# Loading all token tiles at once, normalising them in place on ScalarE, and passing keys, queries, maxima and heads through DRAM in few DMAs

## The chip, the cores and the metric

The kernel runs on one core of a Trainium2 chip. The metric is the device time of one execution in microseconds, as a median of several runs. TensorE is called PE here, VectorE DVE, ScalarE ACT, GpSimd POOL and SyncE SP, as in the profile.

## What is computed

A layer norm, then attention with 32 heads of 16 columns, gated by a bilinear feed-forward layer, all in float32 on 2048 tokens of 512 columns:

```python
xn = _layernorm(x, axis=-1)
# attention: H = 32, Dh = 16
qkv = (xn @ wqkv).reshape(B, S, 3, H, Dh)      # then q, k, v by head
p = softmax(einsum("bhqd,bhkd->bhqk", q, k) * Dh ** -0.5)
s = einsum("bhqk,bhkd->bhqd", p, v) @ wo
# gate: F = 1792
h = (xn @ w_gate) * (xn @ w_up)
g = silu(h @ w_down)
return x + s * g
```

## The kernel before

Most products are made from float32 values split in a high part (rounded) and a low part (the remainder); a product is then three matmuls: high by high, high by low, low by high. Tokens stand in 16 tiles of 128 (`tt`), four to a chunk of 512 (`c`). Heads go in 8 groups of four (`g`); two groups come out of one projection of 128 columns (`m`). One unit of attention `i` is a group of heads with a chunk of queries, 32 units; each has 16 rounds, one for each tile of keys, so there are 512 rounds.

The main loop runs over the rounds. In each, `expo` makes four transposed score tiles (one for each head) and their exponentials on ACT, `score` makes four score tiles of a later unit for their maxima (`LEAD`, 21 rounds ahead), `pv` multiplies the exponentials with the values, and a `Filler` runs a share of the remaining projections, the feed-forward layer and the ending. A score contracts over 48 rows: for each head the keys are (high, low, high) of 16 rows each and the queries (high, high, low). Two rows more carry the negative maxima (high and low) on the queries' side against ones on the keys' side. Heads j = 0, 2 stand at partitions 0 to 49 and j = 1, 3 at 64 to 113 of the tiles `ks` and `QS`.

`qk_proj` and `proj_pair` make keys and queries; `qk_high` (L243) rounds the result on ACT, `qk_out` (L248) makes the low part on DVE and stores both: for each of the three groups of rows (`r`) one DMA to `KD` or `QD` in DRAM, laid out by head and row. `load_q` (L465) and `load_k` (L474) load them for a unit or a group, one DMA for each head. For the first heads (m = 0; all keys, and the first queries) `qk_out` writes directly from SBUF to `ks` and `QS`, in 12 DMAs of 16 rows. `maxima` (L494) sends the maxima through DRAM in 4 stores and 4 loads; `finish` (L531) stores the normalised heads in 4 DMAs.

Ahead of the main loop stands `early` (L561). It loads the token tiles into `raw_x` (8 places, whose tile later becomes the second keys' tile `ks1`), with the other eight loaded once a place is free; `ln_stats`, `ln_root`, `ln_scale` and `ln_apply` normalise (chunk 0 on DVE, the others on POOL, into tiles `xt`), `ln_turn` transposes on PE and splits into `xh` (ACT) and `xl` (DVE). Then a stream of 264 pieces, one 128-row matmul of 512 columns each, runs with an order written out by hand: keys, queries and values of the first heads, with the norm's steps of later chunks at given places (`at`), and at the places of `EARLY` a group of four scores (84 in all). The PSUM tags there are `s` (4 banks, scores), `x` (2, transposes) and `f` (2, projections).

The order of the instructions on PE, ACT and DVE is that of the program (`manual_schedule`); on SP and POOL a scheduler chooses it. SP issues all DMAs, in its order: one that waits holds those behind it.

Of the kernel before, what the change touches and what calls it, by code (L numbers as in the profile page):

```python
# [36 lines left out]
XBUFS = 7  # L37
EARLY = [44 + 16 * n for n in range(7)] + [156 + 8 * n for n in range(14)]
# [7 lines left out]
def body(ctx, tc, x, wqkv, wo, wg, wu, wd, out):  # L46
# [13 lines left out]
    KD = [dram.tile([8, KB, S], F32R, name=f"KD{m}") for m in range(NG // 2)]  # L60
    QD = [[dram.tile([8, KB, 512], F32R, name=f"QD{m}_{c}") for c in range(NC)] for m in range(NG // 2)]
    XD = [dram.tile([2, P, ND, 512], F32R, name=f"XD{c}") for c in range(NC)]
    MD = [dram.tile([32, P], F32, name=f"MD{i}") for i in range(NG * NC)]
    OD = [dram.tile([D, 512], F32, name=f"OD{c}") for c in range(NC)]
# [10 lines left out]
    nc.gpsimd.memset(V[:, :, DH:H * VW:VW], 1.0)  # L75
    nc.gpsimd.memset(V[:, :, H * VW:], 1.0)
# [65 lines left out]

    def load_x(tt):
        dma(raw_x[:, tt % 8], x[tt * P:(tt + 1) * P])

    def ln_stats(tt):
        c, t = divmod(tt, 4)
        if t == 0:
            norm[c] = [qp.tile([P, 4, 2], F32, name="mv", bufs=2)] + [qp.tile([P, 4], F32, name=n, bufs=2)
                                                                        for n in ("ve", "r0", "e1")]  # L150
        st = qp.tile([P, 6], F32, name="st", bufs=2)
        nc.vector.bn_stats(st, raw_x[:, tt % 8])
        nc.vector.bn_aggr(norm[c][0][:, t], st)

    def ln_root(c):
        mv, ve, r0, e = norm[c]
# [3 lines left out]
    def ln_scale(c):  # L160
        mv, ve, r0, e = norm[c]
# [4 lines left out]
        nc.vector.tensor_tensor(e, r0, e, op=OP.mult)  # L166

    def ln_apply(tt):
        c, t = divmod(tt, 4)
        mv, ve, r0, e = norm[c]  # L170
# [3 lines left out]
        norm[c, t] = xt  # L174

    def ln_turn(tt):
        c, t = divmod(tt, 4)
        xt = norm[c, t]
# [55 lines left out]
    def proj_pair(m, which):  # L234
# [6 lines left out]
        soon(1, lambda: [qk_out(o, hi, m, w, c) for o, hi, (_, w, c) in zip(outs, his, which)])  # L241

    def qk_high(o):  # L243
        hi = qp.tile([P, D], F32, name="xt", bufs=XBUFS).bitcast(F32R)
        fst["high"] = nc.scalar.activation(hi, o, AF.Copy)
        return hi

    def qk_out(o, hi, m, which, c):  # L248
        lo = qp.tile([P, D], F32, name="xt", bufs=XBUFS).bitcast(F32R)
        nc.vector.tensor_tensor(lo, o, hi, op=OP.subtract)  # L250
        sl = slice(c * 512, (c + 1) * 512)
        heads = slice(0, P)
        three = (hi, hi, lo) if which == 0 else (hi, lo, hi)
        if m == 0 and (which == 1 or c == 0):
            heads = slice(64, P)
            for j in range(4):
                for r, src in enumerate(three):
                    at = slice(64 * (j % 2) + r * DH, 64 * (j % 2) + (r + 1) * DH)
                    dmar(QS[0][at, j // 2] if which == 0 else ks[0][at, j // 2, sl], src[j * DH:(j + 1) * DH])
        dst = QD[m][c] if which == 0 else KD[m][:, :, sl]  # L260
        for r, src in enumerate(three):
            dmar(dst[heads.start // DH:, r * DH:(r + 1) * DH], src[heads])
# [87 lines left out]
    def o_split(c, tiles):  # L350

        for d, (oh, ol) in enumerate(tiles):
            n = P if c < NC - 1 or d < ND - 1 else 64
            raw = wtile(("w1r", "w0r")[d % 2]).rearrange("p d q -> p (d q)")
            dma(raw[:n], OD[c][d * P:d * P + n])
# [105 lines left out]

    def load_q(i):
# [3 lines left out]
        if i:  # L466
# [4 lines left out]
    def load_k(g):  # L471
        for j in range(4):
            b = 64 * (j % 2)
# [275 lines left out]
```

## Time and profile before

| | us |
|---|---|
| median of 3 runs (lowest, highest) | 1872.29 (1871.79, 1874.9) |
| profiled execution | 1870.86 |
| its span, first to last instruction | 1869.1 |
| PE busy | 1811.5 |
| DVE busy | 1489.6 |
| ACT busy | 1244.3 |
| POOL busy | 528.7 |

A profile has one execution's instructions with their times. PE is its matmuls, PEld its weight loads, which overlap with them. "Idle before" is an engine's idle time ahead of an instruction, with what ended it. PEclk is the share of the full TensorE clock that was granted. SPq means SP issuing DMAs.

### The profile page before, as it was taken

To read this page: it belongs to the slowest core of one execution; us is meant where nothing else is said; L and a number is where in the kernel's file an instruction comes from. 1 tells how busy PE (TensorE), PEld (TensorE's weight loads), DVE (VectorE), ACT (ScalarE), POOL (GpSimd) and SP (SyncE) were. 2 spreads that over 40 slices of the span, in tenths; PEclk is the share of its full clock that TensorE was granted. 3 is DMA by queue.
4 is the path that set the end of the run, shared out by engine and by line. 5 is a ranking of instruction groups with operands and counts; after the bars stand their busy time and mean duration, and the time that the engine had idled before them with its cause. 6 is when DMAs were issued, how large, how long until landed. Compare 5 with 4: busy or idle time off the path is not lost.

```text
span 1869.1 us, 34764 instructions
## 1 busy us (share of the span) xinstructions
PE 1811.5 (97%) x13560; PEld 1000.1 (54%) x13560; DVE 1489.6 (80%) x2461; ACT 1244.3 (67%) x2401; POOL 528.7 (28%) x549
## 2 busy tenths in 40 slices
PE   4799999999999999999999999999999999999998
PEld 3465555555555555555555555555555555555555
DVE  5478888888888888888888888888888888888822
ACT  1116777777777777777767677776777777767664
POOL 4120000042331324313322342331325314223451
PEclk8799999999999999999999999999999999999999
DMA  4231554441113122312113221130124111111232
GB/s 152 65 81 61 193 167 124 113 115 45 52 36 69 50 85 64 80 28 64 46 41 75 100 64 36 53 72 24 58 81 111 41 36 46 45 47 41 100 130 100
DMA packets 122504, 139.77 MB, mean 75 GB/s; under 512 B 18084, under 2 KB 79524, under 8 KB 119460
## 3 DMA queue, kind: packets, MB, share of 16 engines
q1 hardware_dynamic: 122340, 137.55, 25.5%
q8 instruction: 107, 1.75, 0.4%
q14 instruction: 57, 0.47, 0.1%
HBM read 93.98 MB, written 41.42 MB: 72 GB/s over the span
## 4 chain that ended last, share of the span: by engine, by line
PE 92%; ACT 2%; DVE 2%; SPq 1%; DMA 1%; issue 1%; POOL 0%; DVEq 0%; POOLq 0%; ACTq 0%
PE pv L528 26%; PE t L517 21%; PE s L490 10%; PE y L212 6%; PE u L212 5%; PE u L216 4%; PE g L212 4%; PE g L216 4%; PE y L216 3%; PE p L212 2%; PE p L216 1%; PE z L216 1%; PE z L212 1%; ACT e L519 1%; SPq L55 1%
## 5 line engine op out<-in xcount | busy, mean ns | idle before, releaser
L492 DVE TENSOR_REDUCE mx<-s 128x1 f32<-128x512 f32 x2048 | 1312.3, 684 | 269.5 <-PE s L490 147.3
L519 ACT ACTIVATE e<-t 128x512 f32<-128x512 f32 x2048 | 1111.7, 595 | 412.8 <-PE s L490 213.6
L490 PE MATMUL s<-ks,qs 48*128 48x512 f32 x2048 | 714.0, 429 | 16.4 <-DMA qs<-xt 16.3
L517 PE MATMUL t<-qs,ks 50*128 50x512 f32 x2048 | 715.1, 428 | 7.2 <-ACT e L519 5.7
L517 PEld LDWEIGHTS t<-qs,ks 50*128 50x128 f32 x2048 | 346.3, 185 | 521.9 <-ACT e L519 497.0
L528 PE MATMUL pv<-e,V 128*32 128x512 f32 x4096 | 545.5, 605 | 0.0
L490 PEld LDWEIGHTS s<-ks,qs 48*128 48x128 f32 x2048 | 338.5, 185 | 39.5 <-DMA qs<-xt 15.8
L127 POOL CAST w0h<-w0r 128x512 fp32r<-128x512 f32 x60 | 36.8, 613 | 563.0 <-PE u L212 277.2
L528 PEld LDWEIGHTS pv<-e,V 128*32 128x32 f32 x4096 | 81.0, 108 | 154.4 <-issue 145.7
L324 POOL CAST dh<-wdr 128x512 fp32r<-128x512 f32 x56 | 33.7, 613 | 294.4 <-PE y L216 259.9
L541 POOL TENSOR_TENSOR on<-tr,rc 128x256 f32<-128x256 f32 x28 | 17.5, 625 | 261.8 <-DVE rc L539 251.5
L216 PE MATMUL u<-fh,w0h 64*128 64x512 f32 x224 | 88.2, 394 | 0.0
L216 PE MATMUL y<-dh,hh 64*128 64x512 f32 x224 | 88.1, 393 | 0.0
L212 PE MATMUL u<-fh,w0l 64*128 64x512 f32 x224 | 87.9, 392 | 0.0
L212 PE MATMUL g<-fh,w1l 64*128 64x512 f32 x224 | 87.7, 392 | 0.0
L216 PE MATMUL g<-fl,w1h 64*128 64x512 f32 x224 | 87.7, 392 | 0.0
L212 PE MATMUL u<-fh,w0h 64*128 64x512 f32 x224 | 87.7, 392 | 0.0
L216 PE MATMUL g<-fh,w1h 64*128 64x512 f32 x224 | 87.7, 391 | 0.0
L212 PE MATMUL u<-fl,w0h 64*128 64x512 f32 x224 | 87.7, 391 | 0.0
L212 PE MATMUL g<-fh,w1h 64*128 64x512 f32 x224 | 87.6, 391 | 0.0
L212 PE MATMUL y<-dh,hh 64*128 64x512 f32 x224 | 87.6, 391 | 0.0
L212 PE MATMUL g<-fl,w1h 64*128 64x512 f32 x224 | 87.5, 391 | 0.0
(234 smaller groups left out, 2959.9 us busy)
## 6 DMA issues: line engine op xcount, KB each, us to landing
w1r<-in_wg_dram SPq DMA_DIRECT2D x56, 256.0 KB
w0r<-in_wu_dram SPq DMA_DIRECT2D x56, 256.0 KB
wdr<-in_wd_dram SPq DMA_DIRECT2D x56, 256.0 KB
qs<-QD SPq DMA_DIRECT2D x124, 96.0 KB
QD<-xt SPq DMA_DIRECT2D x45, 256.0 KB
ks<-KD SPq DMA_DIRECT2D x28, 384.0 KB
KD<-xt SPq DMA_DIRECT2D x36, 256.0 KB
ks<-in_x_dram SPq DMA_DIRECT2D x16, 256.0 KB
```

Source lines behind the costliest of these rows:

```text
L55: nc.sync.dma_start(dst.bitcast(F32), src.bitcast(F32))
L127: nc.gpsimd.tensor_copy(hi, raw)
L212: nc.tensor.matmul(outs[k], l[LOWER], r[LOWER], start=k == 0 and n == 0, stop=(stop or k == 0) and n == len(low) - 1, skip_group_check=k == 1)
L216: nc.tensor.matmul(outs[1 - k], l[UPPER], r[UPPER], start=k == 0 and m == 0, stop=(stop or k == 0) and m == len(high) - 1, skip_group_chec ...
L324: nc.gpsimd.tensor_copy(dh[:, i], raw)
L490: nc.tensor.matmul(o, QS[i][b:b + KB, pr, t * P:(t + 1) * P], k[b:b + KB, pr, kc * 512:(kc + 1) * 512], start=True, stop=True)
L492: nc.vector.tensor_reduce(MX[i][:, j, t, kc:kc + 1], o, axis=AX.X, op=OP.max)
L517: nc.tensor.matmul(o, k[b:b + KR, pr, kt * P:(kt + 1) * P], QS[i][b:b + KR, pr], start=True, stop=True)
L519: nc.scalar.activation(e, o, AF.Exp, scale=DH ** -0.5)
L528: nc.tensor.matmul(fst["pv"][32 * j:32 * j + 32], V[:, kt, h0:h0 + 32], es[j], start=kt == 0, stop=kt == NT - 1)
L541: (nc.vector if late else nc.gpsimd).tensor_tensor(on[:, :, 0:DH], tr[:, :, 0:DH], rc.to_broadcast([P, 16, DH]), op=OP.mult)
```

## The change

All 16 token tiles are loaded at the start: eight to `raw_x`, the other eight to the first 512 columns of the last eight tiles of `V`, which get their values later; the values' weights are loaded between them. A tile is normalised in place: two on DVE, the other 14 by one ACT instruction with a scale and a bias for each row (a further small DVE operation makes the bias). High and low parts of a projection stand in one tile and go to DRAM in two DMAs of 128 rows, in an order of rows (head, column, group of rows) in which one DMA can load two heads. The first heads' keys and queries go through DRAM as the others do. A unit's queries come in 2 DMAs instead of 4, its maxima go in 1 and come back in 2 instead of 4 and 4, its heads are stored in 1 instead of 4 (with the padding of each head to 32 rows). The 21 groups of early scores stand at places 66, 75, ..., 246 instead of 44 to 140 by 16 and 156 to 260 by 8; the norm's steps and the order of the stream move.

```diff
-XBUFS = 7
-EARLY = [44 + 16 * n for n in range(7)] + [156 + 8 * n for n in range(14)]
+HBUFS = 3
+EARLY = [66 + 9 * n for n in range(21)]
...
+    def tokens(tt):
+        return raw_x[:, tt] if tt < 8 else V[:, tt, 0:D]
...
+        nc.vector.scalar_tensor_tensor(mr, mv[:, :, 0], -1.0, e, op0=OP.mult, op1=OP.mult)
...
     def ln_apply(tt):
-        xt = qp.tile([P, D], F32, name="xt", bufs=XBUFS)
-        (nc.gpsimd if c else nc.vector).tensor_scalar(xt, raw_x[:, tt % 8], mv[:, t, 0:1],
-                                                      e[:, t:t + 1], op0=OP.subtract, op1=OP.mult)
+        xt = tokens(tt)
+        if tt < 2:
+            nc.vector.tensor_scalar(xt, xt, e[:, t:t + 1], mr[:, t:t + 1], op0=OP.mult, op1=OP.add)
+        else:
+            nc.scalar.activation(xt, xt, AF.Identity, bias=mr[:, t:t + 1], scale=e[:, t:t + 1])
...
+    def qk_out(o, hl, m, which, c):
+        nc.vector.tensor_tensor(hl[:, 1], o, hl[:, 0], op=OP.subtract)
+        dst = QD[m][c] if which == 0 else KD[0][c] if m == 0 else KD[m][:, :, c * 512:(c + 1) * 512]
+        both, one = (slice(1, 3), 0) if which == 0 else (slice(0, 2), 2)
+        dmar(dst[:, both], hl)
+        dmar(dst[:, one], hl[:, 0])
...
+    def two(ap, e):
+        return ap.rearrange("(p e d) r t -> e (d r) p t", e=2, d=DH)[e]
...
-            for j in range(4):
-                b = 64 * (j % 2)
-                dmar(q[b:b + KB, j // 2], QD[g // 2][c][4 * (g % 2) + j])
+        for e in range(2):
+            dmar(q[64 * e:64 * e + KB], two(QD[g // 2][c][64 * (g % 2):64 * (g % 2) + 64], e))
+    def load_k(g, cs=range(NC)):
+        heads = slice(64 * (g % 2), 64 * (g % 2) + 64)
+        for e in range(2):
+            k = ks[g % 2][64 * e:64 * e + KB]
+            if g < 2:
+                for c in cs:
+                    dmar(k[:, :, c * 512:(c + 1) * 512], two(KD[0][c][heads], e))
+            else:
+                dmar(k, two(KD[g // 2][heads], e))
...
-            for b in range(4):
-                dma(md[b], mt[32 * b:32 * b + 32])
+            dma(MD[i].rearrange("f (b q) -> b f q", b=4), mt)
...
-        for j in range(4):
-            h0 = (4 * g + j) * DH
-            dma(OD[c][h0:h0 + DH], tn[32 * j:32 * j + DH])
+        dma(OD[c][4 * g:4 * g + 4], tn)
...
+        raws = [etile() for _ in range(ND)]
+        for d in range(ND):
+            dma(raws[d], wqkv[d * P:(d + 1) * P, 2 * D:])
+        for tt in range(8, NT):
             load_x(tt)
...
-        wv = split_rows(wqkv[:, 2 * D:], [etile() for _ in range(ND)], [etile().bitcast(F32R) for _ in range(ND)],
-                        [etile().bitcast(F32R) for _ in range(ND)], nc.sync, True)
-        load_q(0)
+        wv = [[etile().bitcast(F32R) for _ in range(ND)] for _ in range(2)]
+        for d in range(ND):
+            nc.scalar.activation(wv[0][d], raws[d], AF.Copy)
+            nc.gpsimd.tensor_tensor(wv[1][d], raws[d], wv[0][d], op=OP.subtract)
         def k(c):
-            return qk_proj(wk, 0, 1, c, "f")
+            yield from qk_proj(wk, 0, 1, c, "f")
+            load_k(0, [c])
...
-        for c, (stats, root, scale, apply, turns) in {1: ((0, 2, 4, 6), 8, 10, 12, (36, 48)),
-                                                      2: ((26, 28, 30, 32), 34, 38, 74, (96, 108)),
-                                                      3: ((112, 116, 120, 126), 128, 132, 134, (144, 156))}.items():
+        for c, (stats, root, scale, apply, turns) in {1: ((0, 2, 4, 6), 8, 10, 14, (36, 48)),
+                                                      2: ((26, 28, 30, 32), 34, 38, 40, (72, 84)),
+                                                      3: ((50, 52, 54, 56), 58, 62, 64, (108, 120))}.items():
...
-        gens = [k(0), q(0), v(0, 1), k(1), q(1), v(2, 3, 4), k(2), v(5, 6, 7), k(3), v(*range(8, NT))]
+        gens = [k(0), q(0), v(0, 1), k(1), q(1), v(2, 3), k(2), v(4, 5), k(3), v(*range(6, NT))]
```

## Rows read from the trace of the kernel before

**Rows 1.** The page's part 1: busy time, share of span, instructions by engine.

```profile
PE 1811.5 (97%) x13560; PEld 1000.1 (54%) x13560; DVE 1489.6 (80%) x2461; ACT 1244.3 (67%) x2401; POOL 528.7 (28%) x549
```

**Rows 2.** Busy time by stretch; the columns are named in the first line.

```profile
core 0: us, PE busy (x) PEld busy (x) DVE busy (x) ACT busy (x) POOL busy (x), PEclk, DMA share, GB/s
...
16.10:32.90 16.80, 8.41 (x25) 6.18 (x25) 7.10 (x16) 3.59 (x7) 9.23 (x9) 0.87 0.41 127
32.90:42.00 9.10, 8.65 (x28) 6.49 (x28) 2.76 (x6) 0.00 (x0) 7.71 (x4) 0.68 0.35 98
42.00:62.00 20.00, 3.69 (x7) 1.67 (x7) 5.79 (x16) 1.67 (x4) 0.00 (x0) 0.59 0.28 72
62.00:100.40 38.40, 34.90 (x149) 24.40 (x147) 24.70 (x48) 7.93 (x15) 10.41 (x6) 0.90 0.25 67
100.40:112.20 11.80, 10.44 (x40) 7.58 (x40) 4.61 (x9) 3.27 (x6) 6.11 (x3) 0.72 0.18 49
112.20:149.70 37.50, 36.16 (x153) 23.35 (x153) 33.81 (x57) 6.08 (x11) 1.91 (x2) 1.00 0.35 71
149.70:1790.00 1640.30, 1634.33 (x12637) 884.51 (x12637) 1384.76 (x2267) 1174.44 (x2267) 459.36 (x487) 1.00 0.25 71
1790.00:1869.10 79.10, 70.57 (x512) 43.06 (x512) 15.41 (x25) 43.24 (x86) 27.71 (x27) 0.97 0.34 117
```

**Rows 3.** Waits of PE, 0 to 150 us: total, times, longest.

```profile
PE s L490 <- DMA qs<-xt: 16.3, 4, 13.9
...
PE v L189 <- DVE xt L250: 8.8, 2, 8.3
...
PE xT L181 <- POOL xt L172: 3.3, 2, 2.4
```

**Rows 4.** SP in order of time: start, duration, what was issued.

```profile
41.05 7.58 SPq L55 DMA_DIRECT2D ks<-xt  x12
...
50.54 8.70 SPq L55 DMA_DIRECT2D qs<-xt  x12
...
81.07 5.54 SPq L55 DMA_DIRECT2D QD<-xt  x3
91.90 1.75 SPq L55 DMA_DIRECT2D qs<-QD  x4
```

**Rows 5.** The chain that ended last: start, share of the chain, what.

```profile
25.88 3.72 DMA e<-in_wqkv_dram
...
33.68 0.43 PE v L191
...
58.66 1.95 DMA qs<-xt
...
126.75 0.67 PE s L490 x4
...
127.85 0.23 PE v L191
...
129.46 0.79 PE s L490 x4
```

**Rows 6.** Operations by line: count, duration ns lowest/median/highest, first and last start.

```profile
L135 ACT ACTIVATE e<-e x4: 629/630/633, 19.1 to 29.6; 128x512 fp32r<-128x512 f32 x4
...
L152 DVE BATCH_NORM_STATS2 st<-ks x16: 660/662/694, 3.2 to 95.7; 128x6 f32<-128x512 f32 x16
...
L185 DVE TENSOR_TENSOR xl<-xT,xh x12: 681/692/692, 44.0 to 109.7; 128x512 fp32r<-128x512 f32 x12
```

**Rows 7.** Instructions in order of time: start, duration, operation [idle before, releaser].

```profile
85.30 1.04 PE L181 MATMUL xT<-ident,xt 128*128 128x128 f32 x8
...
100.39 1.12 PE L181 MATMUL xT<-ident,xt 128*128 128x128 f32 x4 [2.40 <-POOL xt L172]
...
149.12 1.28 ACT L519 ACT_TABLE_LOAD   x1
...
149.72 0.46 PE L517 MATMUL t<-qs,ks 50*128 50x512 f32 x1 [1.26 <-ACT V L272]
```

**Rows 8.** Groups of instructions, 127 to 149.7 us: busy, mean ns, idle before.

```profile
L492 DVE TENSOR_REDUCE mx<-s 128x1 f32<-128x512 f32 x32 | 19.7, 682 | 2.5 <-PE s L490 2.5
```

More of the change, by code (lines that the diff above doesn't have):

```diff
@@ L58, in body @@
     keep = ctx.enter_context(tc.tile_pool(name="keep", bufs=1))
-    KD = [dram.tile([8, KB, S], F32R, name=f"KD{m}") for m in range(NG // 2)]
-    QD = [[dram.tile([8, KB, 512], F32R, name=f"QD{m}_{c}") for c in range(NC)] for m in range(NG // 2)]
+    KD = [[dram.tile([P, 3, 512], F32R, name=f"KD{m}_{c}") for c in range(NC)] if m == 0 else
+          dram.tile([P, 3, S], F32R, name=f"KD{m}") for m in range(NG // 2)]
+    QD = [[dram.tile([P, 3, 512], F32R, name=f"QD{m}_{c}") for c in range(NC)] for m in range(NG // 2)]
     XD = [dram.tile([2, P, ND, 512], F32R, name=f"XD{c}") for c in range(NC)]
     MD = [dram.tile([32, P], F32, name=f"MD{i}") for i in range(NG * NC)]
-    OD = [dram.tile([D, 512], F32, name=f"OD{c}") for c in range(NC)]
+    OD = [dram.tile([H, 32, 512], F32, name=f"OD{c}") for c in range(NC)]
     YD = [dram.tile([P, 4, D], F32, name=f"YD{c}") for c in range(NC)]
@@ L74, in body, with ones_columns @@
     V = keep.tile([P, NT, VCOLS], F32, name="V")
-    nc.gpsimd.memset(V[:, :, DH:H * VW:VW], 1.0)
-    nc.gpsimd.memset(V[:, :, H * VW:], 1.0)
+    def ones_columns(tts):
+        nc.gpsimd.memset(V[:, tts, DH:H * VW:VW], 1.0)
+        nc.gpsimd.memset(V[:, tts, H * VW:], 1.0)
+    ones_columns(slice(0, 8))
     on = keep.tile([P, 16, 32], F32, name="on")
@@ L141, in body @@
     norm = {}
+    def tokens(tt):
+        return raw_x[:, tt] if tt < 8 else V[:, tt, 0:D]
     def load_x(tt):
-        dma(raw_x[:, tt % 8], x[tt * P:(tt + 1) * P])
+        dma(tokens(tt), x[tt * P:(tt + 1) * P])
     def ln_stats(tt):
@@ L240, in proj_pair @@
         his = [qk_high(o) for o in outs]
-        soon(1, lambda: [qk_out(o, hi, m, w, c) for o, hi, (_, w, c) in zip(outs, his, which)])
+        soon(1, lambda: [qk_out(o, hl, m, w, c) for o, hl, (_, w, c) in zip(outs, his, which)])
     def qk_high(o):
[L244 to L255, printed above, removed]
-            for j in range(4):
[L257 to L262, printed above, removed]
+        hl = qp.tile([P, 2, D], F32R, name="hl", bufs=HBUFS)
+        fst["high"] = nc.scalar.activation(hl[:, 0], o, AF.Copy)
+        return hl
+    def qk_out(o, hl, m, which, c):
[4 more added lines that the diff above has]
+        dmar(dst[:, one], hl[:, 0])
     def v_proj(w, tt, tag):
@@ L352, in o_split @@
         for d, (oh, ol) in enumerate(tiles):
-            n = P if c < NC - 1 or d < ND - 1 else 64
+            heads = 8 if c < NC - 1 or d < ND - 1 else 4
+            n = heads * DH
             raw = wtile(("w1r", "w0r")[d % 2]).rearrange("p d q -> p (d q)")
-            dma(raw[:n], OD[c][d * P:d * P + n])
+            dma(raw[:n], OD[c][8 * d:8 * d + heads, 0:DH])
             nc.gpsimd.tensor_copy(oh[:n], raw[:n])
@@ L504, in rest @@
             nc.vector.transpose(mt, mm.rearrange("p j s t -> p (j s t)").bitcast(F32))
-            md = MD[i].rearrange("f (b q) -> b f q", b=4)
-            for b in range(4):
-                dma(md[b], mt[32 * b:32 * b + 32])
-            for j in range(4):
-                row = 64 * (j % 2) + KB
-                dma(QS[i][row:row + 2, j // 2].bitcast(F32), MD[i][8 * j:8 * j + 8].rearrange("(s t) q -> s (t q)", s=2))
+            dma(MD[i].rearrange("f (b q) -> b f q", b=4), mt)
+            md = MD[i].rearrange("(p e s t) q -> e s p (t q)", p=2, e=2, s=2)
+            for e in range(2):
+                row = 64 * e + KB
+                dma(QS[i][row:row + 2].bitcast(F32), md[e])
         soon(wait, rest)
```

28 lines of the change are left out of this document (9 added, 19 removed).

## The prediction

> **What bounds the kernel now.** I read the page's engine shares first: the matmul engine is busy for 1811.5 of 1869.1 us [rows 1], so at most 58 us of idle time and what the clock takes are to be had, unless matmuls go away, and none does. Then the table of stretches [rows 2], which says where. From 149.7 to 1790 PE is busy 1634.3 of 1640.3 us at clock 1.00: nothing to gain there. From 1790 on 8.5 us are idle, at the end. The rest lies before 149.7, in the early stage (keys, queries and values of the first heads, 84 first scores). From 16.1 to 149.7 its stretches leave 8.4, 0.5, 16.3, 3.5, 1.4 and 1.3 us idle, 31.4 together, and in four of them the granted clock is 0.59 to 0.90. The list of waits [rows 3] names the owners: 16.3 us for the queries' rows by DMA, 8.8 us for VectorE's low part of the first keys, 3.3 us for GpSimd's normalised tokens.
>
> How each comes about: SP's order of issues [rows 4] shows twelve key DMAs from 41.05 (7.58 us) and, after three more stores, twelve query DMAs from 50.54 (8.70 us), with the landing 1.95 us behind the last [rows 5]. The first score can't start before. The 8.8 us hang on the V weights: the chain shows the last rows landing after 3.72 us from 25.88 [rows 5]; ScalarE's copies of them stand in its order ahead of the copy of the first keys, and VectorE's subtraction, which frees the PSUM bank that the values want, stands behind that.
>
> **What the low clock costs.** It has two levels, so a granted clock of c is the low one for 2(1-c) of a stretch. PE fell to it after the idle times: in 32.9 to 42 for 5.8 us, in 42 to 62 for most of 3.7 busy us, in 62 to 100.4 for 7.7 us, in 100.4 to 112.2 for up to 6.6 us [rows 2]. A piece (one 128-row matmul of 512 columns; the early stream has 264) takes 0.43 us there and 0.23 at the high level [rows 5], so about half of such time is lost: 2.9 + 1.5 + 3.8 + 2.5 (part of that stretch is idle) = 10.7 us.
>
> **The change, part by part.**
> Loads: all 16 token tiles and the V weights are issued before any wait. An issue costs some 0.4 us (four query loads in 1.75 [rows 4]) and nothing queued ahead waits. The 8.8 us go if SP's order, which the scheduler chooses, keeps the V weights in front; cover then is the 24 pieces of the first keys and queries. What is late next is GpSimd's four subtractions for V's low parts, with room.
>
> Normalisation: 14 tiles go from GpSimd (12) and VectorE (2) to ScalarE. No ScalarE operation with two per-row operands stands in the trace; nearest is its 128x512 copy from SBUF, 0.630 us [rows 6]. Below: no cheaper, as it moves as much. Above: if Identity needed another function table, a load of 1.28 us [rows 7] twice for three chunks, 7.7 us. I take 0.63 and no load, since Copy runs between the square roots without one. The Trainium skill ("ScalarE: Activation LUTs", What ACT_TABLE_LOAD costs) has 186 ns + 0.833 ns per column and some 93 ns for each pointer operand: an estimate of 0.80 us, by which the eight on the path would cost 1.4 us more and the time would be 1843; no row here shows it. The 3.3 us for GpSimd go (the 2.40 us one stands at 100.39 [rows 7]). The tiny sixth VectorE operation of the scale costs about 0.2 us a chunk.
>
> ScalarE now keeps an order in which a new wait arises. Each chunk's square root stands ahead of the evictions of the transposes before it, and needs four statistics (0.66 us each [rows 6], with the aggregation 3.4 for four). Chunk 2's begin after the low part of the first queries: their pieces end at 23.9 (16.1 + 12 x 0.43 + 12 x 0.23), but ScalarE is in chunk 1's normalisations from about 23.2 (behind that chunk's root and scale) to 25.7, then copies (0.6), and VectorE subtracts (0.7): 27. So statistics to 30.4; root 30.8; evictions of chunk 1's first two tiles to 32; their subtractions (0.69 each [rows 6]) to 32.8; scale to 34; four normalisations of chunk 2 to 36.5; only then the evictions of chunk 1's last two tiles, to 37.7. PE, done with the values at 30.6, waits for a PSUM bank 1.6 us and for those evictions 4.3, before the keys of chunk 1: 5.9 us new idle, and about ten pieces at the low level, 2.0 us. Bounds 0 (the chain catches up by faster statistics) to 12 (all else at its upper bound).
>
> First scores: moved from place 44 to 66 of the stream, with keys and queries through DRAM: 2 stores and 2 loads each. Price of one round trip: the stores' issue 1 to 3.7 us (three took 5.54), 5.3 us from their end (86.6) to the load's issue at 91.90, two load issues 0.9 [rows 4], landing 1.95 [rows 5]: 9 to 12 us. Keys' low part is done at about 23.5 and queries' at 27; SP waits for the keys' stores before it issues the queries', so rows are there at 36 to 46. Place 66 comes at about 44 to 46. I take no wait: the 16.3 us go. Queued behind these waits on SP are only later loads and stores of the same kind.
>
> Scores spread: one group of four each nine pieces. A group with eight pieces takes 126.75 to 129.46 = 2.71 us; nine make 2.94 [rows 5]. VectorE's four maxima are 4 x 0.62 = 2.5 us (32 busy 19.7 in 127 to 149.7, with 2.5 idle [rows 8]), so it is nearly level with PE. Where a pair of transposed tiles falls into a group (four times) it has 2 x 0.65 us more, twice also a low part of keys, while PE has the 1.04 us for eight transposes more [rows 7]: VectorE ends last by some 2 us in all, the maxima over all keys add 0.6, the first group behind chunk 3's scale about 1. New idle 3.5 us.
>
> Main loop: fewer DMAs (maxima 3 for 8, heads 1 for 4, queries 2 for 4, a projection 2 for 3). PE hardly waits there, so 0; the store of heads grows from 128 to 256 KB, and its readers come much later. Three double buffers instead of seven single for the low and high parts: a pair of projections comes every five rounds (24 x 484 / 2328), 17 us at 1719 us for 512 rounds, against some 5 us for a store: 0. GpSimd's ones in V's second half wait for the last transposes, 60 pieces ahead of their first reader: 0. The wait of 1.26 us at 149.72, for the last values and the Exp table, stays [rows 7].
>
> **The sum.** Gone: 8.8 + 16.3 + 3.3 + 10.7 + 0.5 (two normalisations beside VectorE at the start) = 39.6. New: 5.9 + 2.0 + 3.5 = 11.4. Gain 28.2 us. Built up from the front instead (start 15.6; 242 pieces at 0.23 and 22 at 0.43; 21 groups at 0.87; six pairs of transposed tiles at 1.1 with a gap; idle 10.8 with the table's) the first exponential comes at 117 instead of 149.7, a gain of 33; the same count for before comes out 3.5 us short of its trace, so 29 to 30. I take 30. The profiled execution is 1870.9 us (span 1869.1 and 1.8 around it), the median 1.4 above it: 1872.3 - 30 = 1842.
>
> **The rivals.**
> 1. *No wait at chunk 1.* The chain of statistics, root and evictions runs early enough, the clock stays high: 7.9 us less, 1834. For: everything is loaded early. Against: ScalarE's and VectorE's orders are fixed by hand, and now too the square root of chunk 2 holds the evictions.
> 2. *The round trips come late.* Chunks 2 and 3 of the keys have 30 pieces and three groups as cover, about 9.5 us, against a trip of 9 to 12 and a low part that can stand 2.5 us behind maxima. Up to 5 us of waiting each and 9 pieces at the low level (1.8): 2 x 6.8 = 14, 1856. For: the 5.3 us behind the stores. Against: those stores were three with 4 or 8 heads outermost. By the Trainium skill ("DMA: Bandwidth & Descriptors", Why a DMA increments its semaphore by 16 and not by 1) a transfer uses the largest number of engines up to 16 that divides the outermost sizes of both sides; rows fit that, as these stores took 1.8 us to issue each against 0.44 for loads [rows 4]. It lowers this rival here (128 rows outermost) and speaks against the change's store of heads (4 outermost), for which no engine waits.
> 3. *The change doesn't do what it says*: SP's order puts the V weights behind a blocked load, as the weights of later heads now stand between them: 8.8 + 2.9 back, 1854.
> 4. *Scores held by loads of other chunks.* A key load now writes both halves of the tile at once; if scores of older chunks were made to wait for it, three waits of 8 us and 1.8 each: 29, 1871, no change. Against: three stores into interleaved rows of one tensor go out in 5.54 us with no wait between them [rows 4].
> 5. *The clock stays low* through the scores: groups at 9 x 0.43 + 1.1 = 5.0 instead of 2.94 us, 21 x 2.06 = 43: 1885, slower. It decides from about 150 of the 264 pieces at the low level (30 / 0.2). For: the clock fell after every longer idle time. Against: from 112.2 to 149.7, with the same mixture and PE busy 36.2 of 37.5, it was 1.00 [rows 2].
>
> **How the numbers follow.** Forecast 1842 (own range 1834 to 1849): 0.58. Rival 1: 0.11, rival 2: 0.14, rival 3: 0.08, rival 4: 0.04, rival 5: 0.05. Range 1828 to 1858: it holds the forecast and rivals 1 to 3 but for their tails. About 0.2% (3.7 us) is what a measurement tells from no change here. Faster: 0.91 (forecast and rivals 1 to 3); same: 0.04 (rival 4); slower: 0.05 (rival 5).
>
> **What would show it.** First exponential's matmul at 117 to 121 instead of 149.7, and from there to the end 1719 us as now. No PE wait for queries by DMA over 2 us; none for V's first piece; a wait of 4 to 6 us for ScalarE's evictions ahead of the keys of chunk 1, with a clock dip behind it; afterwards groups every 2.9 to 3.0 us and clock 1.00. Waits of scores for DMAs of keys would speak for rival 2 or 4 (4 if the keys waited for belong to a chunk not yet read). Wrong it would be if the stretch behind the first exponential changed by more than 3 us, for which I have no term.

## The result and the profile after

The changed kernel takes 1839.9 us (median of 4, 1838.6 to 1841.7) against 1872.0 us (1870.7 to 1874.9) on the same chip: a ratio of 0.983, interval 0.981 to 0.984. 1842 had been predicted. The profiled execution takes 1841.7 us with a span of 1839.9; against the one of before (1870.9 and 1869.1) that is 29.2 us less, where 30 had been predicted.

Part 1 of the page of the kernel after, to be held against [rows 1]:

```profile
PE 1803.2 (98%) x13560; PEld 992.3 (54%) x13560; DVE 1488.0 (81%) x2463; ACT 1253.7 (68%) x2415; POOL 503.1 (27%) x539
```

PE runs the same 13560 instructions, and its busy time falls by only 8.3 us: that is about the clock's share. ScalarE has 14 instructions more and GpSimd 10 fewer. The span falls by 29.2 us, so idle time of PE gives the other 21. The stretches of the kernel after, with the columns of [rows 2], cut at the first exponential's matmul (118.5):

```profile
0.00:17.70 17.70, 3.92 (x17) 3.04 (x17) 10.54 (x21) 5.76 (x10) 5.59 (x15) 1.00 0.92 319
17.70:38.60 20.90, 15.02 (x64) 11.51 (x64) 12.82 (x36) 11.70 (x22) 5.01 (x4) 0.90 0.40 122
38.60:58.00 19.40, 19.18 (x76) 13.29 (x76) 15.59 (x35) 7.22 (x13) 0.00 (x0) 0.84 0.36 121
58.00:118.50 60.50, 58.44 (x259) 38.64 (x258) 49.01 (x82) 11.05 (x20) 6.21 (x7) 1.00 0.40 90
118.50:1760.00 1641.50, 1635.43 (x12647) 882.96 (x12649) 1384.60 (x2267) 1175.46 (x2269) 459.26 (x488) 1.00 0.26 73
1760.00:1839.90 79.90, 71.17 (x505) 42.84 (x501) 15.42 (x25) 42.52 (x84) 27.07 (x26) 0.96 0.36 118
```

From 17.7 to 118.5 PE is now idle for 8.2 us in all (before, 31.4 from 16.1 to 149.7), and 5.9 of them lie in one stretch, 17.7 to 38.6. The granted clock is lowered in that stretch and in the next (from 34.4 to 44.7 us it is 0.50), and nowhere else ahead of 118.5; PE has nothing to run in 4.2 of these 10.3 us. PE's waits up to 125 us (total, times, longest), as in [rows 3], without that of the first transposes for the tokens at the very start:

```profile
PE p L200 <- ACT xh L195: 4.3, 1, 4.3
PE xT L192 <- DVE xl L196: 1.6, 1, 1.6
PE s L501 <- DMA ks<-KD: 1.1, 2, 0.6
```

The three owners of [rows 3] are gone: no score waits for queries by DMA, no value for V's weights, no transpose for GpSimd. In their place stands the pair that the prediction named, 1.6 us for a PSUM bank and 4.3 us for ScalarE's evictions. The same stretch in order of time (start, duration, operation, in brackets the idle time before it and its releaser):

```profile
8.67 1.26 POOL L133 TENSOR_TENSOR w1l<-w1r,w1h 128x512 fp32r<-128x512 f32 x1
8.75 1.20 DVE L173 TENSOR_TENSOR e<-e,ve 128x4 f32<-128x4 f32 x1
...
9.99 1.33 DVE L174 TENSOR_SCALAR e<-e 128x4 f32<-128x4 f32 x1
...
17.69 0.77 PE L200 MATMUL p<-fh,w1h 128*128 128x512 f32 x1 [0.78 <-ACT fh L195]
...
24.83 0.39 PE L200 MATMUL v<-e,fh 128*128 128x512 f32 x1
...
31.58 0.20 ACT L167 ACTIVATE r<-ve 128x4 f32<-128x4 f32 x1 [4.16 <-DVE ve L166]
31.70 1.06 ACT L195 ACTIVATE xh<-xT 128x512 fp32r<-128x512 f32 x2
33.05 1.25 PE L192 MATMUL xT<-ident,ks 128*128 128x128 f32 x8 [1.58 <-DVE xl L196]
34.70 2.93 ACT L185 ACTIVATE V<-V,mr,e 128x512 f32<-128x512 f32 x4 [1.45 <-DVE mr L176]
37.53 1.05 ACT L195 ACTIVATE xh<-xT 128x512 fp32r<-128x512 f32 x2
38.64 0.79 PE L200 MATMUL p<-xh,w1h 128*128 128x512 f32 x1 [4.33 <-ACT xh L195]
...
118.46 0.49 PE L527 MATMUL t<-qs,ks 50*128 50x512 f32 x1 [0.75 <-ACT V L275]
```

Read it from 31.58 on: the square root of chunk 2, ahead of which ScalarE waited 4.16 us for the statistics; two evictions for chunk 1; four normalisations of chunk 2 (2.93 us); then the other two evictions for chunk 1, and 0.1 us after the second of them PE starts chunk 1's keys. SP's issues of the same time, to be held against [rows 4]:

```profile
24.60 0.81 SPq L55 DMA_DIRECT2D KD<-hl  x2
28.17 0.80 SPq L55 DMA_DIRECT2D QD<-hl  x2
29.08 1.39 SPq L55 DMA_DIRECT2D ks<-KD  x2
32.00 0.78 SPq L55 DMA_DIRECT2D qs<-QD  x2
...
66.43 0.81 SPq L55 DMA_DIRECT2D KD<-hl  x2
...
69.82 0.97 SPq L55 DMA_DIRECT2D ks<-KD  x2
```

Chunk 0's keys and queries of the first heads take 3.8 us of SP in eight issues, where 24 took 16.3 us [rows 4]; the last query load stands at 32.0 instead of at 59. From the stores' end to the dependent load it is 2.6 us for chunk 2's keys (67.24 to 69.82) and 3.7 and 3.0 us for the two pairs at the top, not the 5.3 of before.

### The profile page after: what moved, and what is told of

Read it like the earlier page. It is cut to its first block, busy times and chain, and to the rows that moved or that the text cites. A ratio compares the mean times of both kernels' runs of the same rounds, so it can differ in the third digit from the quotient of the medians.

```text
span 1839.9 us, 34135 instructions
## 1 busy us (share of the span) xinstructions
PE 1803.2 (98%) x13560; PEld 992.3 (54%) x13560; DVE 1488.0 (81%) x2463; ACT 1253.7 (68%) x2415; POOL 503.1 (27%) x539
## 4 chain that ended last, share of the span: by engine, by line
PE 92%; ACT 3%; DVE 2%; DMA 1%; issue 1%; POOL 0%; SPq 0%; DVEq 0%; ACTq 0%; POOLq 0%
PE pv L538 26%; PE t L527 21%; PE s L501 11%; PE y L223 6%; PE u L223 5%; PE g L223 5%; PE u L227 4%; PE g L227 3%; PE p L223 3%; PE y L227 2%; PE z L227 1%; PE p L227 1%; ACT e L529 1%; PE z L223 1%; PE v L200 1%
```

## The experiments

The first theory ("the prediction's"): the gain is the loads issued ahead of all waits (no wait for V's weights, an earlier queue of stores and loads) plus the few DMAs and the later place of the scores; ScalarE's normalisation costs a new wait of some 6 us and a clock dip. Its rivals: the order of rows alone makes the gain; or the new wait costs nothing, because something else would end just as late. What was measured, each kernel against runs of the kernel before on its own chip. "First exponential" is the start of its matmul in the trace, "rest" the span from there on; there is one trace for each kernel. The medians of the kernel before differ by 1.9 us between the chips (1871.8 to 1873.7), so of two kernels on different chips a difference of some 2 us is told by their traces and not by their times.

| kernel | time us | ratio (interval) | first exponential | rest |
|---|---|---|---|---|
| before | 1872.0 | 1 | 149.7 | 1719.4 |
| after | 1839.9 | 0.983 (0.981 to 0.984) | 118.5 | 1721.4 |
| bweights | 1864.2 | 0.995 (0.994 to 0.997) | 140.2 | 1722.1 |
| bloads | 1852.7 | 0.990 (0.988 to 0.991) | 131.3 | 1718.5 |
| direct | 1838.0 | 0.981 (0.980 to 0.983) | 116.8 | 1719.7 |
| scores | 1840.0 | 0.982 (0.981 to 0.984) | 118.6 | 1719.1 |
| pool | 1832.8 | 0.978 (0.977 to 0.980) | 112.7 | 1718.5 |
| later | 1836.8 | 0.981 (0.979 to 0.982) | 114.2 | 1720.4 |
| lows | 1839.5 | 0.982 (0.981 to 0.984) | 118.0 | 1721.3 |
| poolscores | 1836.7 | 0.981 (0.980 to 0.983) | 117.8 | 1718.2 |
| pooldirect | 1835.3 | 0.980 (0.979 to 0.982) | 115.3 | 1718.9 |
| poollows | 1830.6 | 0.978 (0.977 to 0.979) | 108.7 | 1719.5 |
| main | 1844.7 | 0.985 (0.984 to 0.987) | 118.6 | 1724.4 |

The rest lies within 1718.2 to 1722.1 us for all but the last: what the change does to the time it does nearly all ahead of the first exponential. Where the rest is above 1719.7, the clock falls once in the last unit of heads; this and the exception are in the section on main.

### How much the loads carry: bweights and bloads

Both start from the kernel before. The first issues only V's weights early:

```diff
 for tt in range(4, 8):
     load_x(tt)
+raws = [etile() for _ in range(ND)]
+for d in range(ND):
+    dma(raws[d], wqkv[d * P:(d + 1) * P, 2 * D:])
...
-wv = split_rows(wqkv[:, 2 * D:], ..., nc.sync, True)
+wv = [[etile().bitcast(F32R) for _ in range(ND)] for _ in range(2)]
+for d in range(ND):
+    nc.scalar.activation(wv[0][d], raws[d], AF.Copy)
+    nc.gpsimd.tensor_tensor(wv[1][d], raws[d], wv[0][d], op=OP.subtract)
```

> The kernel before with one part of the change: the V weights' rows are loaded ahead of the waiting loads. The 8.8 us wait goes. If SP's queue (token loads that wait for GpSimd's normalisations, then 27 DMAs) sets the first score, that moves from 55.9 to only about 50 to 53: 1864 to 1868 us. If the gains add up as my sum has them (8.8 and 2.9 of low clock): 1859 to 1861.

Measured: 8.4 us less (1864.2 against 1872.6 on its chip). The wait for V's weights is gone from the trace, and the wait for the queries' rows (waits of PE up to 152 us, kernel bweights) is longer than in [rows 3]:

```profile
PE s L490 <- DMA qs<-xt: 18.3, 4, 15.8
```

PE reaches the first score 10 us earlier (32.1 instead of 42.1), but SP's 24 issues end only 8 us earlier (first score at 47.9 instead of 55.9): 16.3 us became 18.3.

The second adds the token tiles of chunks 2 and 3, early and into V's places; GpSimd still normalises, scores and DMAs are as before:

```diff
+for tt in range(8, NT):
+    load_x(tt)
...
-    load_x(tt + 8)
...
-nc.vector.bn_stats(st, raw_x[:, tt % 8])
+nc.vector.bn_stats(st, tokens(tt))
```

> The kernel before with the V weights and all token tiles loaded at the start (the last eight into V's places), everything else as before, normalised by VectorE and GpSimd into other tiles. SP's key DMAs start at about 24 us, the queries' end at 42, first score at about 44 instead of 55.9: 1856 to 1861 us. If the loads alone carry the change: 1840 to 1846. If SP's 27 DMAs alone do: 1866 or more.

Measured: 19.9 us less (1852.7), more than expected and still short of what the whole change gives; the first score comes at 38.4. Waits of PE up to 152 us, kernel bloads:

```profile
PE s L497 <- DMA qs<-xt: 9.9, 4, 7.4
```

The queries' wait shrinks by another 8.4 us, though not one of the 24 DMAs behind it was changed: the token loads no longer stand between them in SP's queue. So the loads alone are some 20 of the 32 us.

### Whether the round trip through DRAM matters: direct

The kernel after, but the first heads' keys and queries go straight to their rows, in 60 small DMAs instead of 20 issues through DRAM (two stores and two loads for each of four chunks of keys and one of queries; the stores stay, for the other heads):

```diff
+if m == 0 and (which == 1 or c == 0):
+    for j in range(4):
+        for r, n in enumerate((0, 0, 1) if which == 0 else (0, 1, 0)):
+            at = slice(64 * (j % 2) + r, 64 * (j % 2) + KB, 3)
+            to = QS[0][at, j // 2] if which == 0 else ks[0][at, j // 2, c * 512:(c + 1) * 512]
+            dmar(to, hl[j * DH:(j + 1) * DH, n])
```

> The changed kernel with the first heads' keys and first queries written directly from SBUF to their places again, 12 DMAs of 16 rows each (60 in all), and no trip through DRAM for them. SP is busy 33 to 42 us with the queries' 12, which land at about 44, when the first scores come anyway; chunks 2 and 3 take 8 to 9 us to land, like the trip through DRAM. If what gained is that no token load blocks SP and that the scores come later, this costs 0 to 4 us: 1839 to 1844 us. If the few DMAs gained: waits of scores for keys of 3 us or more each, 1848 or more.

Measured: 1838.0 us, 1.9 less than the change itself, just below the first range. ScalarE's wait of 4.3 us stands as before, and behind it the rows are there in time either way, so the few DMAs gain nothing in this setting. Of the 1.7 us by which the first exponential comes earlier, 1.1 are the waits for chunk 3's keys, which this kernel doesn't have; behind ScalarE's wait 10 pieces run at the low level instead of 13, which is the other 0.6. The few DMAs pay only where ScalarE's wait is gone (pooldirect, below).

### Whether the later place of the scores matters: scores

```diff
-EARLY = [66 + 9 * n for n in range(21)]
+EARLY = [44 + 16 * n for n in range(7)] + [156 + 8 * n for n in range(14)]
```

> The changed kernel with the 21 groups of scores at the old places (44 to 140 by 16, 156 to 260 by 8). The first group then comes at about 30 us, and the queries' rows land at about 34.5: a wait of 4 to 5 us, but ahead of a wait for chunk 1's evictions that PE has anyway. If the number and the way of the DMAs gained, not the spacing: first exponential at 115 to 120, 1837 to 1843 us. If the spacing carries part of the gain (groups of eight pieces bound by VectorE at 2.83 us, the first group's wait on top): 1845 to 1850.

Measured: no difference (1840.0). Waits of PE up to 120 us, kernel scores:

```profile
PE s L501 <- DMA qs<-QD: 5.6, 2, 5.5
```

The scores now wait 5.6 us for queries, and the keys of chunk 1 wait for ScalarE only 0.7 us instead of 4.3, since that time passes in the other wait. When one wait lies in front of another for the same stretch of time, only the one in front shows. (The low level behind it is shorter too, 4 pieces instead of 13, so "no difference" is a net figure.)

### What ScalarE's normalisation costs: pool and later

The kernel after, with chunks 1 to 3 on GpSimd again and all of chunk 0 on VectorE, but in the form and the places of the change (in place, scale and bias); everything else is as after:

```diff
-nc.scalar.activation(xt, xt, AF.Identity, bias=mr[:, t:t + 1], scale=e[:, t:t + 1])
+(nc.gpsimd if c else nc.vector).tensor_scalar(xt, xt, e[:, t:t + 1], mr[:, t:t + 1], op0=OP.mult, op1=OP.add)
```

> The changed kernel with chunk 0 normalised by VectorE and chunks 1 to 3 by GpSimd again, in place. If ScalarE's normalisations are what holds chunk 1's evictions, GpSimd's 2.08 us for a tile hide and chunk 1's keys start some 3 us earlier than 38.6: 1835 to 1839 us. If the move to ScalarE is itself a gain (GpSimd's tiles late, as in the wait of 3.3 us before, with a low clock behind it): 1844 to 1850.

Measured: 1832.8 us, 7 below the change. PE's longest waits up to 118 us, but for that for the first tokens, are the two for chunk 3's keys, 1.2 us together, and three of 0.7 to 0.8 us. Stretches of the kernel pool (columns as above):

```profile
17.70:38.60 20.90, 19.31 (x81) 14.94 (x82) 17.18 (x47) 7.60 (x17) 11.08 (x12) 1.00 0.40 122
38.60:58.00 19.40, 19.30 (x96) 13.09 (x94) 17.46 (x34) 5.54 (x11) 3.02 (x4) 1.00 0.39 123
```

The wait of 4.3 us falls to 0.7, that of 1.6 us is gone, and the granted clock stays at 1.00 through both stretches. The first exponential comes 5.8 us earlier: that is what ScalarE's normalisation costs ahead of it, and by the times this part of the change costs 7 us.

No transpose waits for GpSimd, but not because a slow engine is hidden, as the expectation had it with 2.08 us for a tile. In this form GpSimd is as fast as ScalarE (0.80 us). Its operations by line, first of the kernel before, then of pool:

```profile
L172 POOL TENSOR_SCALAR xt<-ks,mv,e x12: 2074/2077/2080, 32.3 to 104.4; 128x512 f32<-128x512 f32 x12
L185 POOL TENSOR_SCALAR V<-V,e,mr x8: 767/771/779, 33.7 to 43.2; 128x512 f32<-128x512 f32 x8
```

Both are one operation on a tile with two operands per row. The form of before subtracts, then multiplies, into another tile; that of the change multiplies, then adds, in place. Which of these makes 0.77 us of 2.08 isn't separated by any run. So the run compares two engines at equal cost that differ in what stands behind them: PE's evictions on ScalarE, nothing that PE waits for on GpSimd.

The second kernel leaves the normalisation on ScalarE and moves its places in the stream, so that chunk 1's evictions no longer stand behind chunk 2's square root:

```diff
-{1: ((0, 2, 4, 6), 8, 10, 14, (36, 48)),
- 2: ((26, 28, 30, 32), 34, 38, 40, (72, 84)),
- 3: ((50, 52, 54, 56), 58, 62, 64, (108, 120))}
+{1: ((0, 2, 4, 6), 8, 10, 14, (28, 36)),
+ 2: ((40, 42, 44, 46), 50, 54, 56, (72, 84)),
+ 3: ((58, 60, 62, 64), 68, 70, 76, (108, 120))}
```

> The changed kernel with the norm's steps of chunks 2 and 3 at later places (chunk 1's transposes at 28 and 36 instead of 36 and 48; chunk 2's statistics from 40, root 50, scale 54, normalising 56; chunk 3's from 58, 68, 70, 76). If the 4.3 and 1.6 us of PE ahead of chunk 1's keys come from ScalarE's order (root and normalisations of chunk 2 ahead of chunk 1's evictions), both go, and the low clock behind them: first exponential 5 to 8 us earlier than 118.5, 1832 to 1835 us. If VectorE is what bounds there, its later statistics push the first groups of scores by as much: gain under 2 us, 1838 to 1841.

Measured: 1836.8 us. Stretches of the kernel later, and one of its waits of PE:

```profile
17.70:38.60 20.90, 20.90 (x90) 16.32 (x91) 15.21 (x41) 11.58 (x21) 5.02 (x4) 1.00 0.41 121
38.60:58.00 19.40, 17.32 (x69) 11.34 (x68) 16.63 (x35) 7.97 (x15) 0.00 (x0) 0.91 0.38 123
```

```profile
PE s L501 <- DVE mx L503: 1.2, 1, 1.2
```

The wait for the evictions is entirely gone (PE busy 20.90 of 20.90 us), but the next stretch loses 2.1 us of idle time and some clock: on VectorE chunk 3's statistics (36.4 to 42.1) now stand ahead of the maxima of the first scores, which PE has ready from 37.0 on, and the next scores wait for the maxima. So the first exponential comes 4.3 us earlier, less than the 5.9 of the waits alone, and 1.5 later than in pool. Both theories were half right: the order was the cause of the wait, and moving it hands part of the work to a place where VectorE has no time to spare.

### Whether the two other parts pay once that wait is gone: poolscores and pooldirect

Each is pool with one more part undone, by the diffs of scores and of direct.

> The run with GpSimd's normalisation (first exponential at 112.7 us, 1832.8 us) with the groups of scores at the old places. With ScalarE's normalisations the old places cost nothing, as a wait of 5.5 us for the queries' rows lay beside the wait for chunk 1's evictions. If that was its cover, it is bare here: 5.5 us and some low clock, first exponential at 117 to 120, 1837 to 1841 us. If the places don't matter for another reason (the later groups make up for it): 1831 to 1835.

> The run with GpSimd's normalisation with the first heads' keys and queries written directly from SBUF in 60 DMAs. With ScalarE's normalisations this cost nothing: the queries' rows landed at about 44, before place 66 at 45.7. Here place 66 comes at 39: if the few DMAs gain where the first scores are early, a wait of 4 to 5 us and a low clock, 1836 to 1840 us; and no wait for chunk 3's keys (1.2 us here). If the way of the rows doesn't matter at all: 1830 to 1833.

Measured: 3.9 and 2.4 us over pool (on another chip; in the traces the first exponential comes 5.1 and 2.6 us later). The waits of PE of the kernel poolscores, then of pooldirect, up to 120 us:

```profile
PE s L501 <- DMA qs<-QD: 3.9, 2, 3.5
```

```profile
PE s L509 <- DMA qs<-hl: 2.4, 2, 1.5
```

The same edits that cost nothing behind ScalarE's wait now have a wait of their own that nothing covers, with a low clock behind it (0.59 and 0.71 from 38 to 48 us, 1.00 in pool). So the later place of the scores and the order of rows are each worth something, but only with the normalisation on GpSimd. For the order of rows it is less than the 3 to 7 us expected, as a net figure: this kernel has neither pool's 1.2 us of waits for chunk 3's keys nor the low clock behind them.

### Why the first keys start late: lows and poollows

After has its first keys at 17.69, 1.55 us later than before. In the timeline above two VectorE operations on 128x4 elements (L173, L174) last 1.20 and 1.33 us, beside GpSimd's two subtractions of 1.26 us; elsewhere the same two lines take 0.16 and 0.17. To tell the neighbour from the operations themselves, the two subtractions went to VectorE, behind the second and the fourth transposed tile:

```diff
-nc.gpsimd.tensor_tensor(lo, raw, hi, op=OP.subtract)
+late.append(lambda: nc.vector.tensor_tensor(lo, raw, hi, op=OP.subtract))
...
 for tt in range(4):
     ln_turn(tt)
+    if tt % 2:
+        lows[tt // 2]()
```

> The changed kernel with the low parts of the first two weights on VectorE behind chunk 0's first evictions, instead of on GpSimd while VectorE works out the scale. There two small VectorE operations took 1.20 and 1.33 us instead of 0.16 to 0.17. If GpSimd's subtractions beside them cause that, they shrink, and the first keys start at 15.5 to 16.3 instead of 17.7: 1837 to 1839 us. If the loads that land then cause it, they stay long and the time is 1840 to 1842.

Measured: 1839.5 us, no change. The same two operations and the first keys in order of time, kernel lows:

```profile
8.34 0.62 POOL L132 CAST w0h<-w0r 128x512 fp32r<-128x512 f32 x1 [0.20 <-DMA w0r<-in_wqkv_dram]
8.35 0.62 DVE L176 TENSOR_TENSOR e<-e,ve 128x4 f32<-128x4 f32 x1
...
9.00 0.17 DVE L177 TENSOR_SCALAR e<-e 128x4 f32<-128x4 f32 x1
...
15.54 0.77 PE L203 MATMUL p<-fh,w1h 128*128 128x512 f32 x1 [0.78 <-ACT fh L198]
```

The delay is gone and the keys start 2.15 us earlier, so the neighbour on GpSimd was its cause. The ends say the same: in after the two operations end at 9.95 and 11.32, GpSimd's two subtractions beside them at 9.93 and 11.15; what is left of the first one in lows, 0.62 us, ends at 8.97, with a GpSimd copy beside it that ends at 8.96. ScalarE's chain comes earlier with it: its wait is still 4.3 us, but chunk 1's keys start at 37.60 instead of 38.64, and the first scores at 43.70 instead of 45.99, since 6 of these keys' pieces run at the low level instead of 13. Of these 2.3 us 1.9 are lost again further on, and not in the wait that the expectation spoke of. The chunk 3 keys' wait is 0.70 and 0.66 us instead of 0.53 and 0.57, and behind it the clock falls, which it doesn't in after. The stretch of the kernel lows:

```profile
85.00:95.00 10.00, 8.64 (x32) 5.08 (x31) 5.41 (x10) 1.16 (x2) 0.78 (x1) 0.83 1.09 158
```

At 0.83, 3.4 of the 10 us are at the low level; half of that, 1.7, is lost. With the 0.3 of longer waits this is the 1.9 us, and 0.4 us of gain are left in the first exponential (118.0).

The same edit on top of pool:

> GpSimd's normalisation and the low parts of the first two weights on VectorE together. The low parts alone brought the first keys 2.1 us forward (15.5 for 17.7) but the time by under 1 us. If the wait for chunk 1's evictions swallowed that, it comes through here: first exponential at 110 to 111, 1829 to 1832 us. If VectorE bounds the first 50 us, it is the same as without: 1832 to 1834.

Measured: 1830.6 us, first exponential at 108.7, 4.0 earlier than in pool, more than expected. Chunk 1's keys start 2.0 us earlier (31.95 instead of 33.99). The wait for chunk 3's keys is 0.8 us instead of 1.2, and here the clock stays at 1.00 behind it, while pool has 0.90 and 0.92 in 76 to 85 and 85 to 95, 3.4 us at the low level and some 1.7 lost. By its trace this is the fastest kernel of the study, 3.0 us of span below pool; the times alone don't tell the two apart (0.978 both), as they ran on different chips. It is 9 us below the change and 41 below the kernel before.

### What the fewer DMAs of the main loop do: main

The kernel after, with maxima and heads stored and loaded in as many DMAs as before:

```diff
-dma(MD[i].rearrange("f (b q) -> b f q", b=4), mt)
-for e in range(2):
-    dma(QS[i][row:row + 2].bitcast(F32), md[e])
+for b in range(4):
+    dma(md[b], mt[32 * b:32 * b + 32])
+for j in range(4):
+    dma(QS[i][row:row + 2, j // 2].bitcast(F32), MD[i][8 * j:8 * j + 8].rearrange(...))
...
-dma(OD[c][4 * g:4 * g + 4], tn)
+for j in range(4):
+    dma(OD[c][4 * g + j, 0:DH], tn[32 * j:32 * j + DH])
```

> The changed kernel with the main loop's merged transfers apart again: maxima in 4 stores and 4 loads, heads in 4 stores without padding. PE hardly waits there, so no change: 1837 to 1842 us, the stretch behind the first exponential within 2 us of 1721. If the merged transfers matter in the main loop: 3 us or more either way.

Measured: 4.8 us slower than the change (1844.7), and 5.1 slower than lows on the same chip. Not in the loop: from the first exponential to the start of the last unit of heads this kernel differs by 0.2 us from before. The loss lies in the last 80 us. Order of time there, first the kernel after, then main:

```profile
1762.20 1.62 SPq L52 DMA_DIRECT2D out_dram<-hh  x2
...
1764.83 1.06 SPq L52 DMA_DIRECT2D hh<-YD  x2
...
1769.57 0.69 DVE L383 TENSOR_TENSOR hh<-z,hh 128x512 f32<-128x512 f32 x1 [14.45 <-DMA hh<-YD]
```

```profile
1762.61 1.14 SPq L52 DMA_DIRECT2D qs<-MD  x4
1763.80 0.36 SPq L52 DMA_DIRECT2D out_dram<-hh  x1
1766.69 0.34 SPq L52 DMA_DIRECT2D hh<-YD  x1
...
1771.25 0.50 PE L223 MATMUL z<-fh,hl 64*128 64x512 f32 x1 [2.48 <-DVE hh L383]
```

Output tiles are stored, and their places in SBUF reloaded for the next sum, which VectorE needs before PE gets a bank back. In main four small loads of maxima (1.14 us) stand between the two output stores on SP, the reload starts at 1766.7 instead of 1764.8, PE waits 2.5 and 1.3 us instead of 1.5 and 0.5, and the clock falls for longer. That these loads are the cause is read from the order of the issues; no run moved them alone. The 10 us from the start of the last unit on in before, after and main:

```profile
1799.30:1809.30 10.00, 8.32 (x64) 5.00 (x62) 2.80 (x5) 5.66 (x12) 2.56 (x2) 1.00 0.54 188
1768.00:1778.00 10.00, 7.96 (x48) 4.23 (x48) 3.45 (x6) 3.80 (x9) 2.50 (x2) 0.83 0.61 208
1768.00:1778.00 10.00, 6.18 (x28) 2.84 (x24) 1.38 (x2) 2.39 (x5) 2.54 (x2) 0.72 0.64 213
```

In the profiles the last unit, from its first transposed score to its last, takes 51.4 us in before, 53.7 in after and 56.7 in main, which is 3.0 of main's 4.8 us over after; the rest is not traced to a place, and after's profile is the slowest of its four runs. PE's wait there is 1.7 us in before, 1.5 and 0.5 in after, 0.9 and 0.4 in pool. After and pool have the same instructions there, so the 2.2 us that after takes more than before can't be laid to the fewer DMAs: they go with the clock. Of the kernels with after's ending direct, scores, pool, poolscores and pooldirect stay at 1.00 in this unit and take 51.2 to 51.8 us; later, lows, poollows and after have 0.83 in some 10 us of it and take 52.6 to 53.7. So does bweights (53.5), with the ending of before. Main lies outside both groups. What decides whether the clock falls there was not tried.

## Why the prediction was right

**The main steps held.** First exponential at 118.5 (117 to 121 predicted), no wait for V's first values, none for queries by DMA, a new wait of 1.58 and 4.33 us at chunk 1 (1.6 and 4.3 predicted) with the low level behind it, the places with plain groups 2.9 to 3.0 us apart (2.94). The one later table load is the Exp table's, at 119.03 (149.12 before), so Identity brought none: the upper bound of 7.7 us was void. The gain is the sum of what was to go; rivals 1, 3, 4 and 5 are excluded by the trace: the wait is there, V's values start at 24.83 right behind the queries, scores wait for key loads only 1.1 us in all, and the clock is 1.00 from 58 on. The forecast gain of 30 lies between the 29.2 us of the profiles and the 32.1 of the medians.

**Terms that were off, and why the sum held.**
- *The normalisation* was taken at 0.63 us, the copy's time. Operations by line of the kernel after:

```profile
L185 ACT ACTIVATE V<-V,mr,e x8: 799/802/814, 34.7 to 49.1; 128x512 f32<-128x512 f32 x8
```

 0.80 us, so four take 2.93 instead of the 2.5 of the prediction. The figure that the Trainium skill gives ("ScalarE: Activation LUTs", What ACT_TABLE_LOAD costs) led to an estimate of 0.80, and the trace agrees. The wait came out right all the same (4.33 for 4.3), because both of its ends came late by as much: the evictions end at 38.6 where 37.7 was reckoned, and PE is done with the values at 31.5 instead of 30.6. Both stand behind a start that came 1.6 us later than the 16.1 from which this part of the prediction counts. That it agrees to 0.03 us is luck; that it is there, and why, is not.
- *The start* was set at 15.6 (0.5 us better than before); it came at 17.69. The step that failed is "two normalisations beside VectorE at the start", which left out what GpSimd's subtractions do to VectorE's tiny operations (lows: 2.15 us). In lows the first pieces take 0.63 us until between 20.2 and 20.6, as in after, so the earlier keys run slowly and the values start only 1.25 us earlier (23.58 instead of 24.83).
- *VectorE in the scores* was to cost 3.5 us. From 58 to 118.5 PE is idle 2.06 us in all: 1.1 for DMAs of keys, 0.75 ahead of the first exponential. But the list of idle times doesn't show all. Scores in order of time, kernel after:

```profile
71.67 1.58 PE L501 MATMUL s<-ks,qs 48*128 48x512 f32 x4
75.47 0.72 PE L501 MATMUL s<-ks,qs 48*128 48x512 f32 x4
```

 The second group has its four scores in 0.72 us; in the first they come as VectorE's maxima free the banks, in gaps of 0.1 us and less. Four groups without transposes or waits for keys (at 53.66, 57.50, 71.67 and 103.59) take 3.83, 3.59, 3.80 and 3.18 us instead of 2.94: 2.6 us in all, where "VectorE ends last" had 3.5. The groups with a pair of transposed tiles take 3.8 us, which is PE's own time: 0.87 for a pair, not 1.1.
- *The low clock* was set at 22 pieces, 4.4 us: 12 at the start and 10 behind the wait. In the trace slow pieces (0.56 us or more) stand 6 times from 17.69 on and 13 times from 38.64 on: 19 pieces, 3.8 us. Half of the time at a low granted clock would be 5.2 us, too much, as PE is idle in 4.2 of it; and the slow pieces at the start aren't in the granted clock at all.

 The terms of the count from the front add up to 116.4, not 117. Against it went the start with 2.1 us, for it the clock with 0.6 and the transposes with 1.1; idle time and VectorE together are the 10.8 that it has. So the start and the other two nearly cancel, which is luck, and the trace has 118.5; the last 1.7 us aren't traced.
- *Rival 2* occurs in miniature: 0.53 and 0.57 us for the keys of chunk 3. The trip from store to load took 2.5 to 3.7 us instead of 5.3; with it a round trip is cheap. What rival 2 reads from the issue times doesn't hold: three stores with four heads outermost took 1.76 us in the kernel before (at 48.68), 0.59 each, less than the 1.85 of those with eight, so these times don't follow the number of engines that it reckons with.

**Where the gain comes from** was not asked sharply enough. The prediction gave the few DMAs and the later scores their share of the 16.3 us. The runs say: the loads alone give 20 us (bloads). For the other 12 the wait for queries has to go, and with ScalarE's wait in the way neither the later place nor the order of rows shows a share of its own (scores and direct lose nothing each; both undone together were not tried); without it they are worth 3.9 and 2.4 us. The normalisation on ScalarE, which the sum charged 7.9 us, costs 7, measured by pool; the sum credits it with the 3.3 us for GpSimd, and pool shows that these go as well with the new form on GpSimd (0.77 us for a tile). That the 2.08 us of before belong to the form and not to the engine, the prediction didn't ask.

**Rest of the span.** "0" for the main loop held: from the first exponential to the last unit it is 1649.8 us before and 1649.7 after. The rest is 2.0 us longer (3 was allowed), with the clock in the last unit. But the fewer DMAs aren't worth 0 in the changed kernel: undoing those of maxima and heads costs 4.8 us, in the last unit. The prediction looked for PE's waits in the loop and didn't ask which stores and reloads the small DMAs stand in front of on SP.

## What to carry to other kernels

Loads that only stand behind waits in a queue cost more than their own lateness, since stores and loads of other work stand behind them; issue them first. Work belongs on an engine behind which nothing stands that the bottleneck waits for: the same normalisation takes 0.80 us on ScalarE and 0.77 on GpSimd, and ahead of ScalarE's evictions it cost 7 us, while on GpSimd it did not show. Before an engine is called slow, try the operation in another form: GpSimd's 2.08 us became 0.77. When two waits end close together, undoing one part shows nothing: take the one in front away first, then measure the others.

## What the runs showed of the hardware that was not expected

- VectorE operations on 128x4 elements took 1.20 and 1.33 us beside GpSimd subtractions of 128x512 (1.26 us each), and 0.62 and 0.17 with these moved away; the first keys moved by 2.15 us. Each of the long ones ends within 0.2 us of a GpSimd operation beside it. The statistics, 128x512 with one input, keep their 0.66 us beside four such subtractions (19.0 to 21.3 in after).
- GpSimd's normalisation of a 128x512 tile took 2.08 us as subtract and multiply into another tile, and 0.77 as multiply and add in place.
- Waits of nearly the same length were followed by either level of the clock. All four of these kernels wait twice for chunk 3's keys, 1 us apart: after 0.53 and 0.57 us, later 0.64 and 0.62, pool 0.60 and 0.56, lows 0.70 and 0.66. Behind the first two the clock stayed at 1.00, behind the others it fell, and pieces took 0.63 us instead of 0.39 for some 2 us or more (these durations overlap; from start to start it is 0.43 and 0.23). PE's matmuls of scores in order of time, kernel pool:

```profile
80.57 0.47 PE L501 MATMUL s<-ks,qs 48*128 48x512 f32 x1 [0.60 <-DMA ks<-KD]
81.60 0.70 PE L501 MATMUL s<-ks,qs 48*128 48x512 f32 x3 [0.56 <-DMA ks<-KD]
```

 What decides it stays open; the edits around these waits move the result by 1.7 us through it.
- The slow pieces at the start aren't in the granted clock and don't follow PE's start. In pool the clock is 1.00 from 17.7 to 38.6, and its first seven pieces, from 18.25 on, take 0.63 us or more. Pieces shorten from 0.63 to 0.39 us between 20.2 and 20.6 in after, whose first keys start at 17.69, and also in lows, where they start at 15.54; in pool at 21.6, in poollows, with a start at 15.56, at some 19.5. In direct (17.78) and scores (18.44) they take 0.50 us or less from the first on. That gained direct nothing by itself, since its values then wait 0.8 us for VectorE's low part and start at 24.73.
